# A gated convolution and an MLP on one core: k's first chunk loaded first, kv stored with its time permuted, token transfers merged

## The chip, the core and the metric

The kernel runs on one core of a Trainium2 chip. The metric is the time on the device in microseconds (us). A time in this text is the median of a kernel's executions unless a single one is named. The kernel before ran at 240.22 us (three executions, 240.03 to 240.64) before the change was tried. The state of an execution is "fast" or "slow"; for a kernel that ran once it is unknown. Only fast executions are compared. Where stages are compared, their times come from the profiled execution of each kernel and count from the start of its span.

TensorE does matmuls, VectorE (DVE in the profile), ScalarE (ACT) and GpSimd (POOL) do the elementwise work, and PEld is TensorE's loading of weights. PSUM is the memory that the matmuls of these kernels write to; SBUF holds all their other tiles. The granted clock is the share of TensorE's full clock that the profile shows for a stretch.

## The reference, cut to what matters

All arrays are bf16. x is the input A_q, so its load reads in_A_q_dram in the profile. The sequence has S = 2048 steps and D = 512 channels; the MLP is 1376 wide.

```python
k_shift = sum over t of k_pad[:, t:t+S, :] * shift_k[:, 3-t]     # four taps in time
kv = k_shift * v
y  = irfft(rfft(kv_padded) * rfft(ssm_k_padded))[:, :S]          # long convolution, by channel
y  = y + kv * ssm_D
h  = x + layernorm(x) * y
h2 = h + relu(layernorm(h) @ w1) @ w2
```

## The kernel before

It computes the two Fourier transforms by matmuls in two stages. In order of time it (1) transposes ssm_k and makes tables of sines, (2) makes stage 1 of the transform of ssm_k, in eight blocks, between which TensorE makes the four taps with diagonal weights and VectorE multiplies by v, (3) transposes kv into rows, (4) makes stage 2 for ssm_k ("k spectra"), then stage 1 for kv, (5) multiplies the spectra ("products"), (6) transforms back (psi, then pz, which ScalarE copies to zt), and (7) runs gate, layer norm and MLP over four groups of 512 tokens.

The places that the change touches, with cuts:

```python
def _tokens(src2d, t0, nt):                       # four patterns, 32 rows each
    return [bass.AP(..., offset=... + (16*a + t0)*D, ap=[[64*D, 32], [1, nt*D]]) for a in range(4)]
...
nc.sync.dma_start(out=sk[:], in_=A_ssm_k...)      # first on the queue
... shift_k, ssm_D on ScalarE's queue ...
for c in range(4):                                # then chunks of k and v, transposed
    nc.sync.dma_start_transpose(out=kT[c]..., in_=k_d[...])
    nc.sync.dma_start_transpose(out=vT[:, :, CH*c:CH*c+CH], in_=v_d[...])
...
def to_rows(src, q, fl, eng):                     # 8 transposes: weights with a step of 64 elements
    for i in range(8):
        nc.tensor.transpose(out=pst[:, i, :], in_=src[:, :, :, 8*q + i], identity=ident[:])
...
def taps(u):                                      # u: chunk of 512 steps, group of 128 channels
    ... four matmuls with wdiag into ps ...
    vv = vT[:, rg, CH*c:CH*c+CH]
    nc.vector.tensor_tensor(out=vv, in0=ps[:], in1=vv, op=ALU.mult)        # in place
stage1(kfl, a1k, "ADAADADA", two_taps)            # two units of taps after each block
for q in range(8): to_rows(kvv, q, xfl, ...)      # the kv transposes
for kp in range(16): ... 16 k spectra ...
stage1(xfl, a1x, "ADADADAA")                      # then the transform of kv
...
for a, src in enumerate(_tokens(x_d, 0, NT)):     # four loads of x
    nc.sync.dma_start(out=xh[32*a:32*a+32]..., in_=src)
...
for a, dst in enumerate(_tokens(out_d, t, 1)):    # four stores per 128 tokens
    nc.sync.dma_start(out=dst, in_=o[32*a:32*a+32, :])
```

Of the kernel before, what the change touches and what calls it, by code (L numbers as in the profile page):

```python
# [9 lines left out]
ALU = mybir.AluOpType  # L10
BF16 = mybir.dt.bfloat16
F32 = mybir.dt.float32
F32R = mybir.dt.float32r
I32 = mybir.dt.int32
PSUM = bass.MemoryType.PSUM
P = 128
# [32 lines left out]
def _tokens(src2d, t0, nt):  # L49

    D = src2d.shape[1]
    return [bass.AP(tensor=src2d.tensor, offset=src2d.offset + (16 * a + t0) * D, ap=[[64 * D, 32], [1, nt * D]])
            for a in range(4)]
# [3 lines left out]
def kernel(  # L57
# [37 lines left out]
    nc.sync.dma_start(out=sk[:], in_=A_ssm_k.rearrange("(c p) t -> p c t", p=P))  # L95
    wsh = consts.tile([P, DC, KS], BF16, name="wsh")
    nc.scalar.dma_start(out=wsh[:], in_=A_shift_k.rearrange("(r p) j -> p r j", p=P))
    dtab = consts.tile([P, DC, 64], BF16, name="dtab")
    for dp in range(2):
        src = bass.AP(tensor=A_ssm_D.tensor, offset=A_ssm_D.offset + 64 * dp, ap=[[0, 64], [P, DC], [1, 64]])  # L100
        nc.scalar.dma_start(out=dtab[64 * dp:64 * dp + 64, :, :], in_=src)
# [6 lines left out]
    for c in range(4):  # L108
        if c == 0:
            nc.sync.dma_start_transpose(out=kT[c][:, :, 16:CH + 16], in_=k_d[0:CH, :])  # L110
        else:
            nc.sync.dma_start_transpose(out=kT[c][:], in_=k_d[CH * c - 16:CH * c + CH, :])
        nc.sync.dma_start_transpose(out=vT[:, :, CH * c:CH * c + CH], in_=v_d[CH * c:CH * c + CH, :])
# [21 lines left out]

    n1i = early.tile([P, 1], I32, name="n1i")
# [5 lines left out]
    for s in range(0, P, 64):  # L142
# [5 lines left out]
    ident = consts.tile([P, P], BF16, name="ident")  # L148
    nc.gpsimd.memset(ident[:], 0.0)
    nc.gpsimd.affine_select(out=ident[:], in_=ident[:], compare_op=ALU.not_equal, fill=1.0,  # L150
                            base=0, pattern=[[-1, P]], channel_multiplier=1)

# [9 lines left out]
    _sin(f1f[:, 0:32], t1[:, 0:32], 128)  # L162
    _sin(f1f[:, 32:64], t1[:, 32:64], 128, neg=True)
# [6 lines left out]
    _turns(nc, tsn[:], r2[:], n2c[:], 8192, False)  # L170
# [14 lines left out]
    for rg in range(DC):  # L185
        nc.gpsimd.tensor_tensor(out=wdiag[:, rg, :, :], in0=ident[:].unsqueeze(1).to_broadcast([P, KS, P]),
                                in1=wsh[:, rg, :].unsqueeze(2).to_broadcast([P, KS, P]), op=ALU.mult)
# [5 lines left out]
    def to_rows(src, q, fl, eng):  # L193
        pst = psum.tile([P, 8, P], BF16, tag="ps", name="pst")
        for i in range(8):
            nc.tensor.transpose(out=pst[:, i, :], in_=src[:, :, :, 8 * q + i], identity=ident[:])  # L196
        copy(eng, fl[:, :, :, 8 * q:8 * q + 8], pst[:].rearrange("p i (d g) -> p g d i", d=2))
# [7 lines left out]
    def stage1(fl, a_out, engs, between=None):  # L205
        for gb in range(8):
            pss = [psum.tile([P, 8, 64], F32, tag="ps", name=f"ps1_{r}") for r in range(4)]
            for gi in range(8):
                for f, first in ((f1hi, True), (f1lo, False)):
                    for rg in range(4):  # L210
                        rows = slice(32 * rg, 32 * rg + 32)
                        nc.tensor.matmul(out=pss[rg][:, gi, :],  # L212
                                         lhsT=fl[rows, 8 * gb + gi, :, :].rearrange("p d n -> p (d n)"),
                                         rhs=f[rows, :], start=first, stop=not first, tile_position=(32 * rg, 0))
            for rg in range(4):
                j0 = 64 * rg + 8 * gb
                copy(engs[(4 * gb + rg) % len(engs)], a_out[:, :, j0:j0 + 8], pss[rg][:].rearrange("p g c -> p c g"))
            if between is not None:
                between(gb)

    def stage2(ps, a_in, kp, s):

        for kk in range(2):
            k1 = 2 * kp + kk
            w_re, w_im = ((cc, cs), (cn, cc))[s]
            nc.tensor.matmul(out=ps[:, kk, :], lhsT=w_re[:, k1, :], rhs=a_in[:, k1, :], start=True, stop=False,  # L226
                             skip_group_check=True)
            nc.tensor.matmul(out=ps[:, kk, :], lhsT=w_im[:, k1, :], rhs=a_in[:, 32 + k1, :], start=False, stop=True,  # L228
                             skip_group_check=True)


    kfl = early.tile([P, 64, 2, 64], BF16, name="kfl")
    skv = sk[:].rearrange("p c (a b) -> p c a b", b=64)
    for q in range(8):
        to_rows(skv, q, kfl, "DADADADA"[q])
# [11 lines left out]
    a1k = slotA.tile([P, 64, 256], F32R, tag="A", name="a1k")  # L247


    def taps(u):  # L250
        c, rg = divmod(u, DC)
        ps = psum.tile([P, CH], F32, tag="ps", name="pkv")
        for j in range(KS):
            nc.tensor.matmul(out=ps[:], lhsT=wdiag[:, rg, j, :], rhs=kT[c][:, rg, 16 - j:CH + 16 - j],  # L254
                             start=(j == 0), stop=(j == KS - 1))
        vv = vT[:, rg, CH * c:CH * c + CH]
        nc.vector.tensor_tensor(out=vv, in0=ps[:], in1=vv, op=ALU.mult)

    def two_taps(gb):
        taps(2 * gb)  # L260
        taps(2 * gb + 1)

    stage1(kfl, a1k, "ADAADADA", two_taps)
# [6 lines left out]
    kvv = vT[:].rearrange("p r (a b) -> p r a b", b=64)  # L270
    for q in range(8):
        to_rows(kvv, q, xfl, "ADADADAD"[q])
# [4 lines left out]
    dcol = dtab[:].rearrange("p r g -> p (r g)").unsqueeze(2).to_broadcast([P, 256, 2])  # L277
    for kp in range(16):
        ks = slice(2 * kp, 2 * kp + 2)
        ps = [psum.tile([P, 2, 256], F32, tag="ps", name=f"ps2k{s}") for s in range(2)]  # L280
        for s in range(2):
            stage2(ps[s], a1k, kp, s)
        nc.vector.tensor_tensor(out=kf[:, 0, :, ks], in0=ps[0][:].rearrange("p k j -> p j k"), in1=dcol, op=ALU.add)  # L283
        nc.scalar.copy(out=kf[:, 1, :, ks], in_=ps[1][:].rearrange("p k j -> p j k"))  # L284

    a1x = slotA.tile([P, 64, 256], F32R, tag="A", name="a1x")
    stage1(xfl, a1x, "ADADADAA")
# [15 lines left out]
    def product(kp):  # L303
        ks = slice(2 * kp, 2 * kp + 2)
        kfr = kf[:].bitcast(F32)
        ts = []
        for s in range(2):
            u = psum.tile([P, 2, 256], F32, tag=f"u{s}", name=f"u{s}")
            stage2(u, a1x, kp, s)
            usb = prod.tile([P, 256 - NJ, 2], F32, tag=f"usb{s}", name=f"usb{s}", bufs=2)  # L310
            uj = u[:].rearrange("p k j -> p j k")
            nc.scalar.copy(out=usb[:], in_=uj[:, po, :])  # L312
            t = prod.tile([P, 2, 256, 2], F32R, tag=f"t{s}", name=f"t{s}")
            for eng, in0, j in ((nc.vector, uj[:, dv, :], dv), (nc.gpsimd, usb[:], po)):
                n = j.stop - j.start
                eng.tensor_tensor(out=t[:, :, j, :], in0=in0.unsqueeze(1).to_broadcast([P, 2, n, 2]),  # L316
                                  in1=kfr[:, :, j, ks], op=ALU.mult)
            ts.append(t)
        pending.append((kp, ts))
# [23 lines left out]
    for a, src in enumerate(_tokens(x_d, 0, NT)):  # L343
        nc.sync.dma_start(out=xh[32 * a:32 * a + 32, :, :].rearrange("p t d -> p (t d)"), in_=src)
# [39 lines left out]
    for b in range(32):  # L384
        ps = psum.tile([P, 2, 2 * P], F32, tag="ps", name="psi1")
        for i in range(2):
# [4 lines left out]
        copy("ADAADADA"[b % 8], bp[:, 2 * b:2 * b + 2, :, :, :].rearrange("p g a b c -> p g (a b c)"), ps[:])  # L391
# [9 lines left out]
    pzp = pl.push("psZ", bufs=1, space=PSUM)  # L401
    ptp = pl.push("psT", bufs=1, space=PSUM)
    psum = pl.push("psM", bufs=3, space=PSUM)
# [4 lines left out]
    def inv2(q):  # L408
        pz = pzp.tile([P, 4, 4, P], F32, tag="pz", name="pz")
        for l4 in range(4):  # L410
# [11 lines left out]
    def inv2_copy(q, pz):  # L422
        zts[q] = hp.tile([P, 4, D], BF16, tag="zt", name="zt")
        for l4 in range(4):
# [46 lines left out]
    def chain(q):  # L471
        qln = ln1(q)
# [5 lines left out]
    def mlp1(sc, part=slice(0, 512)):  # L478
# [3 lines left out]
        for fc in range(NFC):  # L482
            fsz = min(P, DFF - fc * P)
# [6 lines left out]
    def mlp2(sc):  # L490
        for i in range(4):
# [8 lines left out]
            for a, dst in enumerate(_tokens(out_d, t, 1)):  # L500
                nc.sync.dma_start(out=dst, in_=o[32 * a:32 * a + 32, :])
# [9 lines left out]
    inv2_copy(0, inv2(0))  # L511
    hln = new_rows(0)
    gate(0, [0, 1], qln, hln, on_act=True)
    gate(0, [2, 3], qln, hln, on_act=True)
    pz = inv2(1)
    transposes(0, hln)
    mlp1(0, slice(0, 2 * P))
    transposes(2, hln)
    inv2_copy(1, pz)
    mlp1(0, slice(2 * P, 4 * P))  # L520
    chain(1)
    inv2_copy(2, inv2(2))
    mlp2(0)
    chain(2)
    mlp1(1)
    inv2_copy(3, inv2(3))
    mlp2(1)
    chain(3)
# [34 lines left out]
```

## Time and profile before

| | before |
|---|---|
| median of the first runs | 240.22 us |
| span of the profiled execution, granted clock | 238.6 us, 0.952 |
| busy: TensorE / VectorE / ScalarE / GpSimd | 86% / 65% / 55% / 26% |
| kv transposes start | 39.71 us |
| first product | 74.73 us |
| first pz (inverse, second half) | 124.99 us |
| first matmul of the MLP | 141.08 us |
| pz of the second group | 154.97 us |
| last add | 234.08 us |

The chain of waits is read as start, length, and what the end of the program was waiting for in that time. In the stretch of the taps, from 21.7 to 36.5 us, it belongs to TensorE alone:

```profile
24.84 1.84 PE pkv L254 x8
26.67 0.61 PE ps L212 x64
27.29 1.84 PE pkv L254 x8
```

Each block costs 1.84 + 0.61 = 2.45 us. VectorE multiplies by v beside it. In the table of groups (line, engine, operation, tiles and shapes, count; busy us, mean ns; idle before it) its sixteen products read:

```profile
L257 DVE TENSOR_TENSOR vT<-pkv,vT 128x512 bf16<-128x512 f32 x16 | 10.7, 689 | 1.2 <-PE pkv L254 1.2
```

### The profile page before, as it was taken

How to read it: one execution, taken by the hardware profiler on the slowest of the kernel's cores; microseconds unless marked ns; L12 is line 12 of the kernel's file. 1: busy time of each engine (PE TensorE's matmuls, PEld its weight loads, DVE VectorE, ACT ScalarE, POOL GpSimd, SP SyncE). 2: the span in 40 equal slices, each digit the busy share in tenths (PEclk: the TensorE clock that was granted, in tenths of full speed). 3: DMA queues.
4: the chain of work that ended last, by engine and by line, in shares of the span. 5: the costliest groups of instructions: out<-in, count | busy, mean ns of one | idle time of the engine just before them, and what ended most of it. 6: DMA issues, size and time to landing. Idle time of an engine off the chain costs nothing.

```text
span 238.6 us, 7218 instructions
## 1 busy us (share of the span) xinstructions
PE 206.1 (86%) x3100; PEld 145.8 (61%) x3100; DVE 154.2 (65%) x299; ACT 130.7 (55%) x241; POOL 62.7 (26%) x88
## 2 busy tenths in 40 slices
PE   0486998999767999998989678899999999979992
PEld 0473555999646999978986546764446444434440
DVE  7886986877655989977995882822577257740031
ACT  3779464666775688897992338912262327105500
POOL 6399700000003999975000001020022002200000
PEclk9999999999955899999999779999999999999998
DMA  6999910000000000009992000023200420042011
GB/s 212 286 206 157 190 34 4 3 1 0 3 5 3 3 1 0 3 1 201 195 368 70 3 3 0 3 46 69 61 8 3 93 71 17 0 91 65 23 44 44
DMA packets 30191, 15.45 MB, mean 65 GB/s; under 512 B 25584, under 2 KB 29008, under 8 KB 30032
## 3 DMA queue, kind: packets, MB, share of 16 engines
q1 hardware_dynamic: 29088, 14.93, 28.3%
q8 instruction: 24, 0.39, 0.7%
q10 hardware_dynamic: 1072, 0.07, 0.4%
q14 instruction: 7, 0.06, 0.1%
HBM read 7.08 MB, written 2.10 MB: 38 GB/s over the span
## 4 chain that ended last, share of the span: by engine, by line
PE 79%; ACT 9%; DMA 5%; DVE 4%; issue 2%; SPq 0%; ACTq 0%
PE ps1m L486 16%; PE ps2m L496 15%; PE pz L417 9%; PE psi L389 6%; PE pst L196 5%; PE psy L326 5%; PE pkv L254 5%; PE u L226 4%; PE u L228 4%; DMA sk<-in_A_ssm_k_dram 4%; PE ps L212 3%; PE ps2k L226 3%; PE ps2k L228 3%; ACT zt L425 2%; ACT c2c L174 2%
## 5 line engine op out<-in xcount | busy, mean ns | idle before, releaser
L488 ACT ACTIVATE h1T<-ps1m 128x512 bf16<-128x512 f32 (+3 forms) x55 | 28.0, 515 | 39.3 <-PE ps1m L486 38.5
L486 PE MATMUL ps1m<-hlnT,w 128*128 128x512 bf16 (+3 forms) x220 | 40.5, 346 | 4.5 <-ACT hlnT L508 2.2
L496 PE MATMUL ps2m<-w,h1T 128*128 128x512 bf16 (+1 forms) x176 | 38.7, 379 | 0.0
L486 PEld LDWEIGHTS <-w 128*128 128x128 bf16 (+1 forms) x220 | 22.6, 103 | 22.1 <-issue 5.3
L499 DVE TENSOR_TENSOR o<-ps2m,xh 128x512 bf16<-128x512 f32 x16 | 11.0, 691 | 38.2 <-PE ps2m L496 38.2
L316 DVE TENSOR_TENSOR t<-u,kf 128x704 fp32r<-128x704 f32 x32 | 27.1, 889 | 4.8 <-ACT usb L312 4.8
L496 PEld LDWEIGHTS <-h1T 128*128 128x128 bf16 (+1 forms) x176 | 17.0, 98 | 21.1 <-issue 0.8
L316 POOL TENSOR_TENSOR t<-usb,kf 128x320 fp32r<-128x320 f32 x32 | 28.7, 924 | 3.4 <-ACT usb L312 2.3
L417 PE MATMUL pz<-bp,ecore 32*32 32x128 f32 x1024 | 22.1, 387 | 4.2 <-ACT zt L425 2.2
L434 POOL TENSOR_SCALAR rstd<-mv 128x4 f32<-128x4 f32 x6 | 1.4, 229 | 88.5 <-DVE mv L441 88.5
L417 PEld LDWEIGHTS pz<-bp,ecore 32*32 32x32 f32 x1024 | 15.8, 108 | 9.8 <-issue 2.9
L439 DVE BATCH_NORM_STATS2 st<-xh 128x6 f32<-128x512 bf16 x32 | 19.8, 680 | 0.0
L328 ACT CAST kf<-psy 128x512 fp32r<-128x512 f32 x32 | 18.4, 645 | 1.6
L389 PE MATMUL psi<-dre,kf 128*128 128x256 f32 x64 | 15.8, 288 | 0.9 <-ACT kf L328 0.9
L425 ACT CAST zt<-pz 128x512 bf16<-128x512 f32 x16 | 8.2, 602 | 13.9 <-PE pz L417 13.9
L326 PE MATMUL psy<-t,ipos 128*128 128x512 f32 x48 | 15.8, 390 | 0.0
L389 PE MATMUL psi<-dim,kf 128*128 128x256 f32 x64 | 15.4, 283 | 0.0
L254 PE MATMUL pkv<-kT,wdiag 128*128 128x512 bf16 x64 | 15.2, 381 | 0.0
L196 PE MATMUL pst<-ident,sk 128*128 128x128 bf16 x64 | 6.7, 299 | 9.2 <-DMA sk<-in_A_ssm_k_dram 9.2
L201 ACT CAST a1k<-ps 128x512 fp32r<-128x512 f32 x20 | 10.4, 593 | 6.7 <-PE ps L212 6.7
L283 DVE TENSOR_TENSOR kf<-ps2k,dtab 128x512 fp32r<-128x512 f32 x16 | 11.0, 694 | 3.5 <-PE ps2k L228 3.4
L284 ACT CAST kf<-ps2k 128x512 fp32r<-128x512 f32 x16 | 10.2, 641 | 5.5 <-PE ps2k L228 5.3
(108 smaller groups left out, 410.0 us busy)
## 6 DMA issues: line engine op xcount, KB each, us to landing
sk<-in_A_ssm_k_dram SPq DMA_DIRECT2D x1, 2048.0 KB, 8.4
xh<-in_A_q_dram SPq DMA_DIRECT2D x4, 512.0 KB, 8.6
out_dram<-o SPq DMA_DIRECT2D x64, 32.0 KB, 1.6
w<-in_B_w_dram SPq DMA_DIRECT2D x1, 1376.0 KB, 15.1
w<-in_B_w_dram SPq DMA_DIRECT2D x1, 1280.0 KB, 18.2
hlnT<-hln SPq DMA_TRANSPOSE x12, 2.5
w<-in_B_w_dram SPq DMA_DIRECT2D x1, 96.0 KB, 17.8
dtab<-in_A_ssm_D_dram ACTq DMA_DIRECT2D x2, 32.0 KB, 8.4
```

The costliest lines, as they stand in the source:

```text
L196: nc.tensor.transpose(out=pst[:, i, :], in_=src[:, :, :, 8 * q + i], identity=ident[:])
L226: nc.tensor.matmul(out=ps[:, kk, :], lhsT=w_re[:, k1, :], rhs=a_in[:, k1, :], start=True, stop=False, skip_group_check=True)
L254: nc.tensor.matmul(out=ps[:], lhsT=wdiag[:, rg, j, :], rhs=kT[c][:, rg, 16 - j:CH + 16 - j], start=(j == 0), stop=(j == KS - 1))
L316: eng.tensor_tensor(out=t[:, :, j, :], in0=in0.unsqueeze(1).to_broadcast([P, 2, n, 2]), in1=kfr[:, :, j, ks], op=ALU.mult)
L326: nc.tensor.matmul(out=psy[:], lhsT=m_[:], rhs=t_.rearrange("p j k -> p (j k)"), start=first, stop=not first)
L328: nc.scalar.copy(out=kf[:, s, :, 2 * kp:2 * kp + 2], in_=psy[:].rearrange("p (j k) -> p j k", k=2))
L389: nc.tensor.matmul(out=ps[:, i, :], lhsT=kf[:, c, 4 * m:4 * m + 4, :].rearrange("p r k -> p (r k)"), rhs=d[:].rearrange("p a b -> p (a b)" ...
L417: nc.tensor.matmul(out=pz[32 * a:32 * a + 32, r4, l4, :], lhsT=ecore[rows, rho, n2, :], rhs=rhs, start=(rho == 0), stop=(rho == 1), tile_p ...
L439: nc.vector.bn_stats(out=st[:, t % 4, :], in_=xh[:, t, :])
L486: nc.tensor.matmul(out=ps1[:fsz, :], lhsT=w1[:, c, fc * P:fc * P + fsz], rhs=hlnTs[sc][:, c, part], start=(c == 0), stop=(c == DC - 1))
L488: nc.scalar.activation(out=h1s[sc][:fsz, fc, part], in_=ps1[:fsz, :], func=ACT.Relu)
L496: nc.tensor.matmul(out=ps2[:], lhsT=h1s[sc][:ksz, fc, i * P:(i + 1) * P], rhs=w2[:ksz, fc, :], start=(fc == 0), stop=(fc == NFC - 1))
```

## The change

The intent: TensorE is idle while ssm_k loads (0 us busy of the first 9.15), so a quarter of the taps is to be done in that time; kv is to be stored so that its transposes load contiguous weights (in the kernel before a load from vT with the step of 64 elements takes 202 ns, one of the contiguous diagonals 98); the diagonals move from GpSimd to VectorE so that they are there early. Beyond that the diff interleaves the transform of kv with the second half of the k spectra (a1 in two halves), gives the inverse transform two half-size buffers, moves layer norms ahead, and merges each group of four token DMAs into one. Its core:

```diff
-    return [bass.AP(..., offset=... + (16 * a + t0) * D, ap=[[64 * D, 32], [1, nt * D]]) for a in range(4)]
+    return bass.AP(..., offset=... + t0 * D, ap=[[16 * D, 4], [64 * D, 32], [1, nt * D]])
...
-    nc.sync.dma_start(out=sk[:], in_=A_ssm_k...)                 # was first
+    nc.sync.dma_start(out=wsh[:], in_=A_shift_k...)              # then k's first chunk, then ssm_k
...
+        nc.vector.tensor_tensor(out=wdiag[:, rg, :, :], in0=ident..., in1=wsh..., op=ALU.mult)   # was gpsimd
...
+    kvx = sk[:]...rearrange("p (b r a) -> p r a b", r=DC, a=32)  # time t = 64*a + b; a innermost
+    kvr = sk[:]...rearrange("p (b x) -> p b x", x=P)             # one transpose: 128 contiguous elements
...
+            nc.vector.tensor_tensor(out=kvx[:, rg, 8 * c:8 * c + 8, :], in0=ps[:].rearrange("p (a b) -> p a b", b=64),
+                                    in1=vv.rearrange("p (a b) -> p a b", b=64), op=ALU.mult)
...
+    first = [taps(u) for u in range(DC)]                         # before the transposes of ssm_k
...
+    for rg in range(DC):
+        nc.gpsimd.tensor_copy(out=kvx[:, rg, 0:8, :], in_=vT[:, rg, 0:CH]...)   # first chunk
...
-        to_rows(kvv, q, xfl, "ADADADAD"[q])
+        to_rows(lambda n2: kvr[:, n2, :], q, xfl, "ADADADAD"[q])
...
+    for gb in range(8):                                          # interleaved
+        stage1(gb, xfl, lambda h, j: a1x[:, h, :, j:j + 8], ...)
+        if gb < 4:
+            spectrum_k(8 + 2 * gb)
+            spectrum_k(9 + 2 * gb)
...
-    for a, src in enumerate(_tokens(x_d, 0, NT)):
-        nc.sync.dma_start(out=xh[32 * a:32 * a + 32, :, :]..., in_=src)
+    nc.sync.dma_start(out=xh[:].rearrange("p t d -> p (t d)"), in_=_tokens(x_d, 0, NT))
...
+    pzp = pl.push("psZ0", bufs=2, space=PSUM)                    # inverse in half-size steps
...
+            nc.sync.dma_start(out=_tokens(out_d, t, 1), in_=o[:])  # one store, was four
```

The time of the permuted store is split as t = 64a + b, with a from 0 to 31. An element of kv lies at position 128b + 32r + a, where r is the group of channels. A product of one chunk covers eight values of a and all 64 of b, and runs through b first. So its neighbouring results lie 128 elements, which is 256 bytes, apart.

## The prediction

> **What bounds the kernel now.** I read the clock and busy slices first, then the chain that ended last in order of time, then single tiles and the timelines of VectorE and ScalarE around each gap of that chain. TensorE is 79% of the chain and 86% busy, so the question at each stage is where it waits. The chain of waits in order of time (start us, length us, what):
>
> ```profile
> 0.72 8.38 DMA sk<-in_A_ssm_k_dram
> 9.15 6.76 PE pst L196 x64
> ...
> 16.95 3.98 ACT c2c L174 x2
> ...
> 39.71 6.00 PE pst L196 x64
> ...
> 72.15 2.54 ACT a1x L201 x5
> ...
> 131.31 2.06 ACT zt L425 x4
> ...
> 149.01 1.96 ACT zt L425 x4
> ...
> 212.29 2.45 DMA hlnT<-hln
> ...
> 234.08 0.69 DVE o L499
> ```
>
> Every line that is not PE is time in which TensorE waits: 9.15 us for ssm_k; 4 us for ScalarE's second sine table; 2.5 us (and, before it, the copies of the x transform from 61.1 to 72.1) for the evacuation of a1x; twice 2 us for zt; 2.45 us for the last transposed hlnT; and the stores after the last sum at 234.8, with the span ending at 238.6. In windows of the stretch around the x transform (window, length; PE, PEld, DVE, ACT, POOL busy with counts; granted clock; DMA share, GB/s):
>
> ```profile
> 62.00:64.00 2.00, 1.34 (x88) 0.85 (x71) 1.77 (x3) 2.00 (x5) 0.00 (x0) 1.00 0.03 8
> 66.00:68.00 2.00, 0.77 (x30) 0.48 (x29) 0.96 (x2) 1.58 (x4) 0.00 (x0) 0.50 0.00 0
> 120.00:122.00 2.00, 2.00 (x19) 2.00 (x18) 1.97 (x6) 1.78 (x4) 0.00 (x0) 1.00 1.04 394
> ```
>
> TensorE is under half busy at 66 us and its clock has been halved. The third line is for a transfer rate that I need below. Weights that load from vT with a step of 64 elements against contiguous diagonals, from the views of the two tiles (ns min/median/max):
>
> ```profile
> L196 PEld LDWEIGHTS <-vT x64: 172/202/221, 39.7 to 45.4; 128*128 128x128 bf16 x64
> ```
>
> ```profile
> L254 PEld LDWEIGHTS <-wdiag x64: 95/98/99, 17.6 to 38.3; 128*128 128x128 bf16 x64
> ```
>
> [...] 0.50 from about 66 to 79 us, and the first 24 products' matmuls come every 0.21 us where later ones take 0.12. [...] The new pattern has 4 as its slowest DRAM dimension against 128 partitions[...]. Nothing in the trace of before shows such a DMA; this is my largest doubt.
>
> **The change part by part.** The diff holds much more than its title.
>
> (a) Front. shift_k and k's first chunk go ahead of ssm_k on the one queue. ssm_k now takes 8.4 us from 0.72; a k chunk (0.5 MB) landed about 2.5 us after it. So I put ssm_k at 12.3 and k's first chunk near 6, and v's first chunk, behind both in either order, stays near 14.8. The sixteen first taps (4 x 0.92 = 3.7 us of TensorE, from the pitch of 1.84 us per two units) fit between 7 and 12, when it was idle. Against that, VectorE now makes the diagonals (4 x about 0.5, by the 0.42 us of a plain 128x512 bf16 product), so the first table's turns end near 10 instead of 7.1, and ScalarE's table (4.2) ends near 14.3. The eight sk transposes run 12.3 to 20.2, held up by four banks that the first taps keep until v's first chunk lands and VectorE multiplies (4 x 0.65, to 18.7); the last kfl copy ends near 21.5, where it was 16.9. ScalarE's second table then runs 20.4 to 24.5, the same stall as before but later, and TensorE restarts at about 25.4. Twelve units and six blocks are left: 1.84 + 5 x 2.45 + 0.61 = 14.7, so the last block ends at 40.2 and the kv transposes start at 40.4, 0.7 later than now. They are contiguous: 64 at some 57 ns (eight pt transposes take 0.62 us with their drain) is 3.7 us for 6.0. The k spectrum starts at 44.1 instead of 45.7: **-1.6**. GpSimd copies the first chunk by about 30, long before it is needed.
>
> (b) Spectra and the x transform interleaved. Now: 16 x 0.96 = 15.4 of spectrum, bound by TensorE, then 11.0 of x transform bound by copies, then 2.5 of tail, in all 29 us to 74.7. After: 8 spectra 7.7; four blocks of one transform step and two spectra, each 2 x 0.65 + 2 x 0.67 = 2.65 on VectorE (TensorE 0.61 + 1.93 = 2.54), 10.7; the last four steps with 10 copies on ScalarE at 0.505, 5.2; tail 0.5. That is 24.1: **-4.9**. The layout of a1 in halves is what allows it; no wait is added, as each half is free by then.
>
> (c) Clock. The thin stretch shrinks from 11 to some 5.5 us, which may or may not trip the halving. It cost 24 x 0.09 = 2.2 us, but GpSimd (0.92 x 32 = 29.6 busy of 33.3) then sets the pace. I count **-0.5**.
>
> (d) Front of the inverse. With two buffers of four banks and halves, zt, gate and transforms overlap. From the first pz at 0: halves end at 3.1, 6.2, 9.3, 12.3; gate of tokens 0,1 runs 4.2 to 7.2; zt of 2,3 waits in ScalarE's order for that gate's root (7.5 to 8.6); second gate to 11.6; zt of the second group 11.9 to 14.0; the new small pools overlie those banks, so the pt transposes start at 13.0 and the first MLP at 15.1, against 16.1 now. Then its two halves run without the 1.5 + 2.3 us of waits between them: 6.4 + 0.6 + 5.1 ends at 27.2 against 30.0: **-2.8**.
>
> (e) The last chain. Its first layer norm (2.46 + 0.36 + 1.5 + 1.38 us) moves ahead of the adds of the second MLP, so hlnT is there by 209 where it now holds TensorE from 213.5 to 214.9: **-1.4**.
>
> (f) Stores. The last four issues of 0.42 become one: **-1.0** at the tail.
>
> The sum is -12.2: 228.0 us.
>
> (g) The token DMAs on fewer engines. In the view of the tile, the old load reads so:
>
> ```profile
> L344 SPq DMA_DIRECT2D xh<-in_A_q_dram x4: 354/416/421, 107.2 to 108.6; - x4
> ...
> DMA to landing us min/median/max: 5.5/8.6/11.5
> ```
>
> All four land by about 120, 4 us before VectorE first reads xh at 124.2. On 4 engines: 394 GB/s over 16 is 24.6 each in the weights' window, so 2.1 MB takes 21 us plus 1.5. Issued at about 100.3 (seven earlier) it lands at 123, and VectorE wants it at 117.2; the whole chain of (d) moves by some 5. The last store would take 1.3 us longer at 32 KB an engine and eat (f). That is +5.9: 234 us. [...] I give it 45%[...], because a kernel that is already tuned is unlikely to keep a load that makes its next stage wait.
>
> **The rivals.** First, (g): a transfer that was hidden becomes the wait. For: [...]the shrinking slack. Against: 4 us of slack today, and four DMAs into 32 partitions each reached only some 230 GB/s, which one of 128 partitions on all engines could better. It makes 234. Second, VectorE and ScalarE become the bound of the front: the table is later by 3 us, [...]and the kfl copies alternate behind both. For: ScalarE's 4 us is on the chain already and everything queues in order. Against: TensorE gets 3.7 us of taps done early and has 14.7 us of its own left. If ssm_k lands at 13.5 or the order bites harder, the front loses 2 instead of gaining 1.6: 231 to 232 without (g), 237 with it. Third, TensorE is already so busy that gaps only move: in the product stage GpSimd and TensorE are both nearly full, so a better clock is worth nothing, and the first MLP starts cold again; that takes some 2 off (c) and (d): 230.
>
> **How range and chances follow.** Without (g) I hold 228 with a spread of about 2.5, with it 234 with about 3. Weighted this is 230.7, and I round up to 231. The tenth lowest and highest of that mixture lie near 226 and 237. Faster by 2% means under 235.4: nearly certain without (g), some two thirds with it, hence 0.86. Slower needs several stalls at once.
>
> **What would show it.** (a) kfl's last copy near 21.5, kv transposes starting near 40.4 with weight loads near 100 ns and lasting under 4.5 us. (b) the first product near 68 with VectorE nearly full from 52 to 62. (c) the clock's halved slices gone or fewer. (d) no zt line of 2 us in the chain in front of the first MLP; (e) no hlnT DMA in it. (f) one store at the end. (g) xh landing over 18 us after its issue and a wait of VectorE's statistics for it. The prediction is wrong if the kv transposes start after 43, if xh is late by more than 8 us, or if the interleaved blocks take over 3.2 us each because PSUM banks run out.

## The result and the profile after

The kernel after takes 276.94 us (four executions, 275.99 to 277.24); the kernel before in the same rounds takes 240.22 (three executions, 240.03 to 240.64). A fourth of it, 243.92, is over 1.5% above the fastest, so it counts as slow and is left out; with it the median is 240.43. The ratio is 1.152, with a 95% interval of 1.148 to 1.156: it is slower by 15%. Ratios here are the mean time of one kernel's fast runs over that of the other's of the same rounds, so they are not quite the ratio of the medians quoted. The profiled execution has a span of 274.8 us at a mean clock of 0.888.

The stages show where the time came from (us from the start of the span):

| start of | before | after | added in this stage |
|---|---|---|---|
| kv transposes | 39.71 | 58.85 | +19.1 |
| first product | 74.73 | 90.49 | −3.4 |
| first pz | 124.99 | 140.22 | −0.5 |
| first matmul of the MLP | 141.08 | 179.09 | +22.8 |
| last add | 234.08 | 269.40 | −2.7 |
| end of span | 238.6 | 274.8 | +0.9 |

Two stages lost 42 us, the others together gained 5.7. The chain of waits of the kernel after has pieces of another kind than before:

```profile
3.41 10.09 DMA sk<-in_A_ssm_k_dram
...
27.05 4.76 DVE sk L252 x2
31.82 0.52 DVE a L205
...
38.06 4.62 DVE sk L252 x2
...
58.85 5.76 PE pst L198 x64
...
122.48 40.51 DMA xh<-in_A_q_dram
163.01 2.47 DVE st L469 x4
...
174.94 1.94 ACT zt L455 x4
...
269.40 0.69 DVE o L530
```

Between 27 and 58 us the chain now runs through VectorE: two products that hold it for 4.6 to 4.8 us, then a copy, then the next products. Later a single DMA of 40.5 us stands in it. The groups say the same of the product, and that the transposes' weights did become cheaper (L198 mixes the 64 loads for ssm_k, still with a step, and the 64 for kv; its shortest load takes 97 ns, where the shortest with the step took 168 in the kernel before):

```profile
L252 DVE TENSOR_TENSOR sk<-pkv,vT 128x512 bf16<-128x512 f32 x12 | 28.3, 2545 | 1.1 <-PE pkv L242 1.1
...
L198 PEld LDWEIGHTS <-sk 128*128 128x128 bf16 x128 | 11.5, 166 | 5.1 <-issue 4.1 <-DMA sk<-in_A_ssm_k_dram 1.0
```

The product takes 2545 ns on the same shapes that took 689, and VectorE waited only 1.1 us before the twelve of them, so it sets the pace. The table of waits (who waited for whom: us in total, times, longest) has the other loss:

```profile
DVE st L469 <- DMA xh<-in_A_q_dram: 23.5, 1, 23.5
PE pz L445 <- ACT zt L455: 22.8, 2, 20.8
```

VectorE's first statistics stand 23.5 us for the load of x, and TensorE stands 20.8 us in one piece behind it, because the gate, and then ScalarE's zt, come in that order. In windows (start and end, length; busy us and count of PE, PEld, DVE, ACT, POOL; granted clock; DMA share; GB/s) of both stretches:

```profile
24.00:26.00 2.00, 0.62 (x2) 0.29 (x3) 1.99 (x4) 1.77 (x5) 2.00 (x2) 0.50 1.15 144
150.00:154.00 4.00, 0.00 (x0) 0.00 (x0) 0.00 (x0) 0.00 (x0) 0.00 (x0) 0.50 0.25 66
```

In the second every engine is idle, the DMA share is 0.25, and 66 GB/s move. In the first TensorE is short of work (0.62 us busy of 2.00) and its clock is at 0.50. That the 40.5 us are one transfer is seen in the view of the tile:

```profile
L372 SPq DMA_DIRECT2D xh<-in_A_q_dram x1: 732/732/732, 122.5 to 122.5; - x1
```

### The profile page after: what moved, and what is told of

The parts are those of the page before. It is cut to its first block, busy times and chain, and to the rows that moved or that the text cites. A ratio compares the mean times of both kernels' runs of the same rounds, so it can differ in the third digit from the quotient of the medians.

```text
span 274.8 us, 7155 instructions
## 1 busy us (share of the span) xinstructions
PE 210.0 (76%) x3087; PEld 146.7 (53%) x3100; DVE 176.0 (64%) x307; ACT 129.7 (47%) x239; POOL 67.3 (24%) x88
## 4 chain that ended last, share of the span: by engine, by line
PE 55%; DMA 18%; DVE 18%; ACT 3%; issue 3%; SPq 1%; POOLq 0%; DVEq 0%; ACTq 0%
DMA xh<-in_A_q_dram 15%; PE ps1m L517 14%; PE ps2m L527 14%; DVE sk L252 9%; PE psy L355 5%; PE pz L445 4%; DMA sk<-in_A_ssm_k_dram 4%; PE u L229 3%; PE ps2k L229 3%; PE u L231 3%; PE pst L198 3%; PE ps2k L231 3%; DVE a L205 2%; DVE st L469 2%; PE ps L214 2%
## 5 line engine op out<-in xcount | busy, mean ns | idle before, releaser
L445 PE MATMUL pz<-bp,ecore 32*32 32x128 f32 x1024 | 21.8, 389 | 25.2 <-ACT zt L455 22.8
L469 DVE BATCH_NORM_STATS2 st<-xh 128x6 f32<-128x512 bf16 x32 | 19.8, 680 | 23.5 <-DMA xh<-in_A_q_dram 23.5
L203 ACT CAST a<-ps 128x512 fp32r<-128x512 f32 x38 | 19.8, 596 | 22.6 <-PE ps L214 22.5
L252 DVE TENSOR_TENSOR sk<-pkv,vT 128x512 bf16<-128x512 f32 x12 | 28.3, 2545 | 1.1 <-PE pkv L242 1.1
L242 PE MATMUL pkv<-kT,wdiag 128*128 128x512 bf16 x58 | 19.3, 473 | 9.1 <-DVE wdiag L173 7.1
L205 DVE CAST a<-ps 128x512 fp32r<-128x512 f32 x26 | 17.9, 732 | 3.5 <-PE ps L214 3.5
L214 PE MATMUL ps<-f_hi,kfl 32*128 32x64 bf16 x256 | 8.0, 207 | 12.3 <-DVE sk L252 8.3
L242 PEld LDWEIGHTS <-wdiag 128*128 128x128 bf16 x64 | 6.8, 115 | 18.2 <-DVE wdiag L173 7.4
```

Source lines behind the costliest of these rows:

```text
L203: nc.scalar.copy(out=o, in_=i)
L205: nc.vector.tensor_copy(out=o, in_=i)
L242: nc.tensor.matmul(out=ps[:], lhsT=wdiag[:, rg, j, :], rhs=kT[c][:, rg, 16 - j:CH + 16 - j], start=(j == 0), stop=(j == KS - 1))
L252: nc.vector.tensor_tensor(out=kvx[:, rg, 8 * c:8 * c + 8, :], in0=ps[:].rearrange("p (a b) -> p a b", b=64), in1=vv.rearrange("p (a b) -> ...
L445: nc.tensor.matmul(out=pz[32 * a:32 * a + 32, r4, l4, :], lhsT=ecore[rows, rho, n2, :], rhs=rhs, start=(rho == 0), stop=(rho == 1), tile_p ...
L469: nc.vector.bn_stats(out=st[:, t % 4, :], in_=xh[:, t, :])
```

## The experiments

My theory had two causes that add up: the merged load of x runs on 4 of the 16 DMA engines (the share of 0.25 above; that its slowest dimension of 4 makes it so was an estimate until run 2), and the permuted store makes VectorE the bound of the taps' stretch (2545 ns for a product). The rivals were that the load is slow for another reason than its outer dimension, that the taps' stretch is late because of the new order of the front (ssm_k later, first taps holding PSUM, diagonals on VectorE), and that the product is slow because of how it reads, or by the number of runs it writes, rather than for writing single bf16. Thirteen kernels ran: four on one chip, eight on a second, and the last on a third. The fast executions of the kernel before have a median of 241.26 beside runs 1 to 4, of 239.63 and 239.95 beside the others, and of 240.22 beside the kernel after, so a difference between sessions is good to about 1 us.

**1. The load of x in four again.** This is the kernel after with one edit:

```diff
-    nc.sync.dma_start(out=xh[:].rearrange("p t d -> p (t d)"), in_=_tokens(x_d, 0, NT))
+    for a in range(4):
+        nc.sync.dma_start(out=xh[32 * a:32 * a + 32, :, :].rearrange("p t d -> p (t d)"),
+                          in_=bass.AP(tensor=x_d.tensor, offset=x_d.offset + 16 * a * D, ap=[[64 * D, 32], [1, NT * D]]))
```

> The changed kernel with only xh's load put back to four DMAs of 32 rows. Theory 'four engines': the load is slow because its slowest DRAM dimension is 4, so it runs on 4 of 16 engines. Then xh lands about 9 to 12 us after its issue at 122.5 instead of 40.5, the DMA share after 146 us is near zero, VectorE's statistics no longer wait, the first MLP starts some 15 us after the first pz (140.2) instead of 39, and the time falls by 22 to 24 us to 253 to 255. Rival 'contention': xh is slow because w1 and w2 are loaded beside it; then it lands as late as before and the time stays near 277.

Measured: 252.83 us (ratio 1.049, 1.043 to 1.055). The wait for x is gone: the statistics start at 139.2, before the first pz at 140.0. The edit is worth 276.94 − 252.83 = 24.1 us, about the 23.5 us that VectorE had waited (by the two ratios, each to its own kernel before, it is 24.7).

**2. One load, its DRAM dimensions exchanged.** Same bytes, same single DMA, but 32 as the slowest dimension in place of 4. Rows land in the wrong partitions, so the result is wrong.

```diff
+    nc.sync.dma_start(out=xh[:].rearrange("p t d -> p (t d)"),
+                      in_=bass.AP(tensor=x_d.tensor, offset=x_d.offset, ap=[[64 * D, 32], [16 * D, 4], [1, NT * D]]))
```

> Wrong result on purpose: the same single DMA of the same 128 rows of 16 KB into the same 128 partitions, but with the DRAM dimensions of 4 and 32 exchanged, so 32 is the slowest. Theory 'four engines': 16 engines, DMA share near 1 while it runs, xh lands within 8 to 12 us of its issue, time 251 to 255. Rival 'one DMA of long rows': a single DMA over 128 partitions with 16 KB rows is slow whatever the order; then it lands after some 40 us and the time stays near 277.

Measured: 253.58 us in one run, of unknown state, and no wait for x. The window while x loads:

```profile
124.00:126.00 2.00, 2.00 (x19) 2.00 (x19) 1.97 (x5) 1.92 (x4) 0.66 (x1) 1.00 0.99 426
```

The share is 0.99 where it was 0.25. In the packet records of the kernel after, from 150 to 154 us, there are four packets in flight at 97% of the moments and five at the rest, never fewer; in the kernel before, from 110 to 112, with four loads and a share of 1.06, sixteen to eighteen. One packet counted as one engine, as in the share, that is four of the 16 at work at a time; which four, the records do not say. Merging four loads into one was not the fault; the slowest dimension of 4 was (276.94 us with 4, 253.58 with 32). This one load even moved 426 GB/s where the four of the kernel before moved 213 (110 to 112 us). Why isn't shown, and no run loads the right rows this way.

**3. The permuted store in runs of eight.** The kernel after, with the loops of the product exchanged: a now runs first, so it writes eight neighbours before it steps by 256 bytes. It reads both inputs with a step of 64 elements instead.

```diff
-            nc.vector.tensor_tensor(out=kvx[:, rg, 8 * c:8 * c + 8, :], in0=ps[:].rearrange("p (a b) -> p a b", b=64),
-                                    in1=vv.rearrange("p (a b) -> p a b", b=64), op=ALU.mult)
+            nc.vector.tensor_tensor(out=kvx[:, rg, 8 * c:8 * c + 8, :].rearrange("p a b -> p b a"),
+                                    in0=ps[:].rearrange("p (a b) -> p b a", b=64),
+                                    in1=vv.rearrange("p (a b) -> p b a", b=64), op=ALU.mult)
```

> The changed kernel with the loops of the kv product exchanged: each of the 64 columns is written as a run of 8 adjacent bf16, and both inputs are now read with steps of 64 elements. Same bytes, same instructions. Theory 'scattered writes': each 2-byte write into another 256-byte row costs about 4.7 ns, so with runs of 8 the product falls from 2.55 to 0.7 us, the kv transposes start near 41 instead of 58.9 and the time falls by 15 to 18 us to 259 to 262. Rival 'three-dimensional patterns or reads': the product stays at 2.5 us or more since its reads are now the scattered ones; time 277 or more. Second rival 'GpSimd contention': no change either.

```profile
L252 DVE TENSOR_TENSOR sk<-pkv,vT 128x512 bf16<-128x512 f32 x12 | 12.0, 1036 | 2.9 <-PE pkv L242 2.9
```

Measured: 259.23 us (ratio 1.075), 17.7 less than the kernel after, with the load of x left slow. The kv transposes start at 43.22 and take 3.73 us. So the order of the front is not what made them start at 58.85.

**4. kv in place, as before.** The kernel after without the permuted store: products in place in vT, transposes with the step of 64.

```diff
-    for rg in range(DC):
-        nc.gpsimd.tensor_copy(out=kvx[:, rg, 0:8, :], in_=vT[:, rg, 0:CH].rearrange("p (a b) -> p a b", b=64))
...
-                times_v(u, taps(u))
+                times_v(u, taps(u), place=True)
...
-        to_rows(lambda n2: kvr[:, n2, :], q, xfl, "ADADADAD"[q])
+        to_rows(lambda n2: kvv[:, :, :, n2], q, xfl, "ADADADAD"[q])
```

> The changed kernel with the time-permuted store undone: every kv product goes in place into vT, GpSimd's four copies go, and the transposes read vT with a step of 64 elements as in the kernel before. Theory: all of the front's loss is the store, so the products take 0.69 us, the kv transposes start near 40.5, their 64 take 6.0 us against 5.8, and the time is 259 to 262. If the early taps, the later ssm_k or VectorE's diagonals cost something of their own, the transposes start later than 43 and the time is over 263.

Measured: 259.52 us (ratio 1.080). The product is back to 688 ns, the kv transposes start at 41.86 and take 5.94 us with weight loads of 202 ns. The permuted store as written is worth 276.94 − 259.52 = 17.4 us of loss. What the new order of the front alone does is now visible too: 41.86, against 39.71 to 41.22 in three traces with the old order (the kernel before and runs 8 and 12), so it gains nothing here.

**5. The permuted store in pairs.** With the load of x in four (as in 1), and pairs of neighbours in a written together. An aligned pair of bf16 fills a word of 4 bytes; a product still writes 256 separate runs.

```diff
+            nc.vector.tensor_tensor(out=kvx[:, rg, 8 * c:8 * c + 8, :].rearrange("p (a l) b -> p a b l", l=2),
+                                    in0=ps[:].rearrange("p (a l b) -> p a b l", l=2, b=64),
+                                    in1=vv.rearrange("p (a l b) -> p a b l", l=2, b=64), op=ALU.mult)
```

> On top of the four loads of xh, the kv product writes its columns as 256 runs of 2 adjacent bf16 (one aligned 4-byte word each) per 512 elements; the shipped loop writes 512 runs of one element (2.55 us), the earlier experiment 64 runs of eight (1.04 us). Theory 'every run costs': the extra over 0.69 us goes with the number of runs, about 3.6 ns each, so 0.69 + 256 x 3.6 ns = 1.6 us. Rival 'half-word writes': only writes of less than a 4-byte word are slow, so pairs take 0.7 to 1.0 us. Time between 238 and 246.

```profile
L252 DVE TENSOR_TENSOR sk<-pkv,vT 128x512 bf16<-128x512 f32 x12 | 8.2, 690 | 3.5 <-PE pkv L242 3.5
```

Measured: 236.06 us in one run, of unknown state. The product costs 690 ns, as if it were contiguous, though it still jumps 256 bytes after each pair. The theory that every run costs has fallen: halving the number of runs did not halve the excess, it removed all of it. TensorE is back at its pace in the chain of this kernel:

```profile
36.77 0.61 PE ps L214 x64
...
39.22 0.61 PE ps L214 x64
```

39.22 − 36.77 = 2.45 us per block, as before.

**6. Both mended, first form.** Load in four as in 1, runs of eight as in 3.

```diff
+    for a in range(4):                                           # as in 1
+        nc.sync.dma_start(out=xh[32 * a:32 * a + 32, :, :]..., in_=...)
...
+            nc.vector.tensor_tensor(out=kvx[:, rg, 8 * c:8 * c + 8, :].rearrange("p a b -> p b a"), ...)   # as in 3
```

> The changed kernel with both faults mended: xh in four loads and kv written in runs of 8. If the two losses found so far are separate and are all of it, the time is the changed kernel's 277 less 24 and less 17.7, 235 us. If they overlap (the late xh hides part of the front's loss), it is above 240.

Measured: 238.18 us, the kernel before 239.63 (ratio 0.992, 0.987 to 0.996). The two losses add nearly: by simple sum 276.94 − 24.1 − 17.7 = 235.1 was due; this kernel is 3 above it and run 5, at 236.06, 1 above, of which the change of chip may be 1. With both mended the change is at or under the time of the kernel before, so there is no third loss of size.

**7. The stores in four as well.** The kernel of 6 with the four old stores:

```diff
-            nc.sync.dma_start(out=_tokens(out_d, t, 1), in_=o[:])
+            for a in range(4):
+                nc.sync.dma_start(out=bass.AP(tensor=out_d.tensor, offset=out_d.offset + (16 * a + t) * D,
+                                              ap=[[64 * D, 32], [1, D]]), in_=o[32 * a:32 * a + 32, :])
```

> As the mended kernel, and the output stores too put back to four of 32 rows. Theory 'four engines' holds for stores as well: with 16 engines the last store lands about 1 us sooner after its issue, but four issues of 0.42 cost 1.3 more, so the tail from the last add to the end goes from 4.7 to about 4 and the time falls by 0.3 to 1. Rival: one issue is always better, so the time rises by about 1.

Measured: 237.43 us (ratio 0.988, 0.983 to 0.993). From the start of the last add to the end of the span it takes 4.5 us, where the single store of 6 takes 4.97. The medians differ by 0.75 us, the intervals overlap; the end of the span is the surer sign.

**8. The title undone.** Kernel 7 with ssm_k first, no leading taps, kv in place and diagonals on GpSimd, so that what is left of the change is the interleaving, the halves of the inverse and the moved layer norms.

```diff
+    nc.sync.dma_start(out=sk[:], in_=A_ssm_k...)                 # first again
-    first = [taps(u) for u in range(DC)]
-        if 0 < gb < 7:
-            for u in (2 * gb + 2, 2 * gb + 3):
-                times_v(u, taps(u))
+            for u in (2 * gb, 2 * gb + 1):
+                times_v(u, taps(u), place=True)
```

> The changed kernel with everything of its title undone (ssm_k first, taps of the first chunk in their old place, kv in place in vT with strided transposes, diagonals on GpSimd) and with loads and stores in fours, so that only the interleaved spectra, the halves of the inverse and the earlier layer norms stay. The plain-store run had its kv transposes start at 41.9 where the kernel before has 39.7, so the theory that the new front order itself costs 2 us gives a start at 39.7 and the first product at 70.5 to 71, and a time of 234 to 236. If the new front order is neutral, the time equals the mended kernel with four stores within 1 us.

Measured: 236.21 us (ratio 0.984, 0.980 to 0.989). This is no worse than kernel 7, which has the whole title with the runs of eight (the intervals overlap). The kv transposes of its profiled execution start at 41.22 rather than the 39.71 of the kernel before; its clock was at 0.56 to 0.59 from 22 to 26 us, where the kernel before has 1.00. Run 12, with the same front but for the store and the transposes of kv, has 1.00 as well. What decides whether the dip comes is not shown.

**9. Four forms of the write, side by side.** One kernel with the load in four, in which each group of channels writes its products in another form. The data of kv is wrong. The comparison with the reference passed all the same, I take it because the convolution's part of the output is small beside x; only the lengths of the products are used.

```diff
+            if rg == 0:    # single bf16 every 4 bytes
+                o = skf[:, 0:1024].rearrange("p (a b x) -> p a b x", a=8, x=2)[:, :, :, 0]
+            elif rg == 1:  # single bf16 every 64 bytes
+                o = skf[:, 0:2048].rearrange("p (b a) -> p a b", a=32)[:, 0:8, :]
+            elif rg == 2:  # contiguous write, both inputs read with a step of 64 elements
+                o = skf[:, 0:512].rearrange("p (b a) -> p b a", a=8)
+            else:          # runs of four every 256 bytes
+                o = kvx[:, rg, 8 * c:8 * c + 8, :].rearrange("p (a l) b -> p a b l", l=4)
```

> Wrong result on purpose: the twelve later kv products write in four forms, one for each group of channels, from its own source line: (0) single bf16 every 4 bytes; (1) single bf16 every 64 bytes; (2) adjacent bf16 in order, but both inputs read with a step of 64 elements; (3) runs of four adjacent bf16 every 256 bytes. Theory 'half-word writes': a bf16 written alone in its 4-byte word is slow whatever the step, so forms 0 and 1 take about 2.5 us, form 3 about 0.7, and form 2 about 1.0, which would be the part that the runs of eight paid for their reads. Rival 'wide step': the 256-byte step is the cost, so form 0 takes 0.7 and form 1 between 0.7 and 2.5. Rival for the runs of eight, 'long runs cost': form 2 takes 0.7.

```profile
L259 DVE TENSOR_TENSOR sk<-pkv,vT 128x512 bf16<-128x512 f32 x3 | 7.2, 2402 | 0.9 <-PE pkv L242 0.7
L266 DVE TENSOR_TENSOR sk<-pkv,vT 128x512 bf16<-128x512 f32 x3 | 3.1, 1030 | 0.3
L262 DVE TENSOR_TENSOR sk<-pkv,vT 128x512 bf16<-128x512 f32 x3 | 3.0, 1007 | 0.0
...
L256 DVE TENSOR_TENSOR sk<-pkv,vT 128x512 bf16<-128x512 f32 x3 | 2.2, 725 | 9.2 <-POOL sk L279 9.2
```

The lines are, in order, every 64 bytes, runs of four, strided reads, every 4 bytes. A single every 4 bytes costs next to nothing (725 ns for 689), one every 64 bytes nearly as much as one every 256 (2402 for 2545). Reading both inputs with the step costs 1007 by itself, so the 1036 of runs of eight is a cost of reading, not of writing, and so is the 1030 of runs of four. The pairs of run 5 read with the same step, two elements at a time, and pay nothing (690); why is not shown. (One run, 248.44 us.)

**10. The slow load put into the kernel before.** The kernel before with only the load of x merged, with 4 as slowest dimension.

```diff
-    for a, src in enumerate(_tokens(x_d, 0, NT)):
-        nc.sync.dma_start(out=xh[32 * a:32 * a + 32, :, :].rearrange("p t d -> p (t d)"), in_=src)
+    nc.sync.dma_start(out=xh[:].rearrange("p t d -> p (t d)"),
+                      in_=bass.AP(tensor=x_d.tensor, offset=x_d.offset, ap=[[16 * D, 4], [64 * D, 32], [1, NT * D]]))
```

> The kernel before with one part of the change alone: xh loaded by one DMA with 4 as its slowest DRAM dimension. Theory 'four engines': it lands some 40.5 us after its issue near 107.3, so at about 148, 23.6 us after VectorE wants it (124.2); the pz of the first group and the second cannot hide that, so the time is 240 + 20 to 24, 260 to 264. Rival 'the old order hides it': under 250.

```profile
DVE st L439 <- DMA xh<-in_A_q_dram: 23.5, 1, 23.5
```

Measured: 262.36 us in one run (state unknown), against 239.95: that part alone costs some 22 us. It was issued at 109.3, where the old loads of x started at 107.2, and the first statistics that need it start at 149.8. The same wait of 23.5 us arises in a kernel with nothing else changed.

**11. The whole change, mended.** Kernel 5 with the stores in four: the title stays, with pairs in place of singles.

```diff
+        nc.sync.dma_start(out=xh[32 * a:32 * a + 32, :, :]..., in_=...)                        # as in 1
+            nc.vector.tensor_tensor(out=kvx[...].rearrange("p (a l) b -> p a b l", l=2), ...)   # as in 5
+                nc.sync.dma_start(out=..., in_=o[32 * a:32 * a + 32, :])                       # as in 7
```

> The changed kernel with its title's parts kept and three things mended: xh in four loads, kv written in pairs, stores in fours. From the single look at pairs (236.1, one store) and the 0.75 us that four stores gave the runs-of-eight kernel: 235 to 236, faster than before by about 2%. If four stores do not help, 236.

Measured: 234.89 us (six executions, 234.0 to 235.83; ratio 0.979, 0.975 to 0.982).

**12. The old front with the permuted store in pairs.** Kernel 8 with the permuted store in pairs and contiguous transposes:

```diff
-                times_v(u, taps(u), place=True)
+                times_v(u, taps(u))                              # pairs, into kvx
...
-        to_rows(lambda n2: kvv[:, :, :, n2], q, xfl, "ADADADAD"[q])
+        to_rows(lambda n2: kvr[:, n2, :], q, xfl, "ADADADAD"[q])
```

> As the last, but with ssm_k first, no leading taps and diagonals on GpSimd as in the kernel before: only the time-permuted store (in pairs) is left of the title. If contiguous transposes are worth the 2.2 us that 64 of them save (5.97 to 3.73) on top of the old front's 236.2, the time is 234. If the new front's early taps are worth something once the store is cheap, this one is slower than the last.

Measured: 234.65 us (six executions, 234.19 to 235.33; ratio 0.978, 0.974 to 0.982). It is the fastest of all, beats both kernels, and is as fast as kernel 11 within the spread. So the early chunk of k, the leading taps and the diagonals on VectorE bring nothing that shows, and the permuted store in pairs brings 236.21 − 234.65 = 1.6 us (the executions of the two kernels do not overlap, the intervals of their ratios just do, and they ran in different rounds). Runs 6, 7, 8, 11 and 12 are all faster than the kernel before, their intervals lying under 1; by 2%, none of them is beyond doubt. A part of why the early taps bring nothing shows in the same window of kernel 11 and then of kernel 12:

```profile
24.00:26.00 2.00, 0.95 (x2) 0.41 (x3) 1.67 (x3) 2.00 (x5) 2.00 (x2) 0.50 0.73 145
```

```profile
24.00:26.00 2.00, 1.95 (x71) 1.09 (x71) 1.77 (x4) 0.98 (x3) 2.00 (x3) 1.00 1.34 241
```

With the early taps ScalarE's second table comes later (it starts at 19.67 in kernel 11, at 16.97 in kernel 12), TensorE is idle from 19.4 to 21.9 us in kernel 11, and its clock is at 0.50 when the blocks start. The kernel after and runs 4, 5 and 6, also with the new front, have 0.50 in this window too. In the old order TensorE is at work with a clock of 1.00 by then in the kernel before and in kernel 12, but not in run 8 (0.56), so the clock is no full answer.

**13. More steps, and pairs across words.** As 9, with other forms; again only the lengths count.

```diff
+            if rg == 0:    # single every 8 bytes
+                o = skf[:, 0:2048].rearrange("p (a b x) -> p a b x", a=8, x=4)[:, :, :, 0]
+            elif rg == 1:  # single every 16 bytes
+                o = skf[:, 0:4096].rearrange("p (a b x) -> p a b x", a=8, x=8)[:, :, :, 0]
+            elif rg == 2:  # single every 32 bytes
+                o = skf[:, 0:8192].rearrange("p (a b x) -> p a b x", a=8, x=16)[:, :, :, 0]
+            else:          # pairs as in 5, shifted by one element: each lies across two words
+                o = skf.rearrange("p (b r a) -> p r a b", r=DC, a=32)[:, rg, 8 * c - 1:8 * c + 7, :]
```

> Wrong data on purpose, as in the forms run (there the comparison with the reference still passed). Single bf16 written every 8 bytes, every 16 and every 32, and pairs of adjacent bf16 at an odd element, so that each pair lies across two 4-byte words. Known so far: single every 4 bytes 0.73 us, every 64 bytes 2.40, every 256 bytes 2.55, aligned pairs every 256 bytes 0.69. Theory 'partial word, each in a line of its own': a half-filled word is cheap while its neighbours in the same 32 or 64 bytes follow, and dear when each write is in a new one; then 8 bytes takes under 1.2 us, 16 in between or low, 32 about 1.5 to 2.4, and the odd pairs, two half-filled words each, about 2.4 or more. Rival 'number of runs or step alone': the odd pairs take 0.7 as the aligned ones do.

```profile
L259 DVE TENSOR_TENSOR sk<-pkv,vT 128x512 bf16<-128x512 f32 x3 | 7.3, 2429 | 0.3
L262 DVE TENSOR_TENSOR sk<-pkv,vT 128x512 bf16<-128x512 f32 x3 | 6.9, 2316 | 0.0
L265 DVE TENSOR_TENSOR sk<-pkv,vT 128x512 bf16<-128x512 f32 x3 | 5.2, 1717 | 0.1
...
L256 DVE TENSOR_TENSOR sk<-pkv,vT 128x512 bf16<-128x512 f32 x3 | 3.9, 1297 | 8.8 <-POOL sk L279 8.8
```

In order: every 16 bytes, every 32, shifted pairs, every 8. The excess over 690 ns is 0.6 us at 8 bytes and 1.6 to 1.9 from 16 bytes on, where the lengths are nearly level: 2429, 2316, 2402 and 2545 ns at 16, 32, 64 and 256 bytes (this run, run 9 and the kernel after). Spread over the 512 singles of a product, an estimate, these are 4.5 to 5.0 ns each; at 8 bytes it is 2.5 (1297 / 512), at 4 bytes 1.4 (725 / 512), and in order 1.3 (689 / 512). The 4.7 ns expected for run 3 is the shortest such product of the kernel after, 2404 / 512. Aligned pairs, which fill whole words, cost nothing here (690 ns every 256 bytes). The shifted pair shows that the place in the words counts, and neither runs nor reads: the same pairs, read alike and written one element off, cost 1717 instead of 690. Why a half-filled word costs more, and more as the step grows to 16 bytes, no trace shows. (One run, 255.74 us.)

## Why the prediction was wrong, and where it was right

It predicted 231.0 (226 to 237) and faster; the kernel is slower, at 276.94. Two of the three marks that it named for its own failure came true: the kv transposes start after 43 (at 58.85), and x is late by more than 8 us (by 23.5). The third, interleaved blocks of over 3.2 us, did not (2.72).

**(a), the front: wrong, by the cost of the product.** The step that failed is "Twelve units and six blocks are left: 1.84 + 5 x 2.45 + 0.61 = 14.7". Up to it the working held: ssm_k was due at 12.3 and landed at 13.5, but the last kfl copy was due near 21.5 and ended at 21.85, and TensorE restarted at 25.15 for 25.4. The 2.45 is the pitch of the kernel before and holds only while VectorE keeps up with products of 0.69 us. The working kept it for the twelve later products although their output pattern had changed to single bf16 every 256 bytes. They measured 2.55. A block then costs two products and the copies of stage 1 on VectorE: 38.06 to 48.96 in the chain is two blocks, 5.45 us each. The blocks took from 25.15 to 58.72, which is 33.6 us, for 14.7. The prediction had itself set 202 ns against 98 for the weights that load with a step and without, but gave the product that now wrote with one no cost. The store moved the stepping walk from TensorE's loads to VectorE's writes (2545 ns for 689). The contiguous transposes did come out as said: 3.73 us for 3.7 in run 3. In the kernel after itself they took 5.76, with the clock at 0.50 for most of it (from 58 to 62 us; 0.71 from 62 to 64).

Even with the product mended, (a) is not there. In run 5 the six blocks run from 25.18 to 41.68, 16.5 us for 14.7; they begin at half clock (0.50 from 24 to 26 us) and come down to a pitch of 2.45 us, and in run 11 the kv transposes start at 41.56 for 40.4. Run 12, with the old order, has them at 40.55. The second rival, "VectorE and ScalarE become the bound of the front", had the right place, for a reason it did not give.

**(g), the load of x: the right cause, its size and its chance wrong.** That the load would run on four engines was an estimate, for which the trace of before showed nothing. The share of 0.25 and the four packets in flight bear it out, and run 2 shows that the dimension decides it (share 0.99 with 32). The mis-sized term is "24.6 each": it came from a window in which sixteen engines were busy at 394 GB/s (share 1.04). Four engines alone moved 66 (share 0.25), which is 16.5 each. The transfer took 40.5 us where the term gave 22.5 (21 plus 1.5, an estimate; the 32 KB stores of the kernel before take 1.6 us from issue to landing). Over its whole length the mean is 2,097,152 bytes / 40.51 us = 51.8 GB/s, less than the 66 of the late window. It was slower beside the weights, queued behind it: the trace's 16 KB packets, the length of x's rows, landed at 47 GB/s from 126 to 140 us, while the weights moved too (share 0.98 to 1.14), and at 65.5 from 142 to 158, when they were through (share 0.26). At 66 GB/s throughout the 2,097,152 bytes would have taken 31.8 us; from the first packet's start to the last landing it was 38.4, so the slower stretch cost some 6.6 by this estimate. Why four engines moved 16.5 each where sixteen moved 26.6 each (run 2) is not shown. The step of judgement that failed is that "a kernel that is already tuned is unlikely to keep a load that makes its next stage wait": it gave 45% to an estimate that runs 1, 2 and 10 bore out in kind. In the kernel after, where (a)'s loss moved the start of the load from the 100.3 foreseen to 122.5 but moved its consumer as well, it cost 24.1 us (run 1); alone in the kernel before, 22 (run 10).

**(b), the interleaved spectra: right in kind, its tail mis-sized.** From the end of the kv transposes to the first product it took 29.0 us before, 25.9 after (64.6 to 90.5) and 25.3 in run 12 (44.30 to 69.58), for the 24.1 predicted: a gain of 3.1 to 3.7 for 4.9. The four interleaved blocks take 2.72 us each for 2.65. What failed is "tail 0.5": ScalarE's last five copies stand in front of the first product as they did before (2.54 us there), in the kernel after and, by its chain, in run 12:

```profile
87.91 2.54 ACT a L203 x5
```

**(c), the clock: nil.** The halved stretch shrank (from 65.6 to 79.3 us before, from 87.0 to 93.9 after), but the clock is still at 0.50 when the products start, and the first products' matmuls are 0.21 us apart as before, for a gain of 0.5.

**(d), the front of the inverse: nil for −2.8.** From the first pz to the pz of the second group it takes 30.0 us before (124.99 to 154.97) and 30.1 in run 12 (120.10 to 150.21), where nothing waits for x. The failed step is "the new small pools overlie those banks, so the pt transposes start at 13.0 and the first MLP at 15.1". In the chain of run 12:

```profile
120.10 4.43 PE pz L441 x190
...
133.90 1.08 ACT zt L451 x2
...
135.02 1.03 PE pt L535 x8
...
137.19 4.43 PE ps1m L513 x20
```

The transposes start 14.9 after the first pz, directly behind ScalarE's last two copies of zt, and the MLP at 17.1, where it was 16.1 before. Its first 20 matmuls take 4.43 us, 0.22 each, twice the 0.11 of the same matmuls in the kernel before at full clock (32 in 3.65 us): the third rival, that "the first MLP starts cold again", is what happened, if cold means the halved clock. The kernel before has 0.50 there as well (142 to 144 us), but in run 12 the clock stays at 0.50 from about 133.5 to 143. The waits between the halves of the MLP did go, and it takes 13.0 us for 13.9, which just pays for the later start.

**(e), the last chain: right.** From the pz of the second group to the last add it takes 79.1 us before (154.97 to 234.08) and 77.4 in run 12 (150.21 to 227.57): −1.75 for −1.4.

**(f), the stores: wrong sign.** From the last add to the end it takes 4.5 us before and in run 7 with four stores, and 4.97 (run 6) to 5.4 (after) with one. (g) had foreseen it in a sentence, "The last store would take 1.3 us longer", an estimate from 24.6 GB/s for an engine; with the issues that it saves, the one store came out 0.5 to 0.9 us longer.

The sum, by runs: the load of x +24.1, the permuted store +17.4 to +17.7, and the rest −5.1 (kernel 11, whose edits mend the two and undo the merged stores, is at 234.89, against 239.95 of the kernel before). 24.1 + 17.5 − 5.1 = 36.5, and 276.94 − 240.22 = 36.7; with sessions that differ by 1 us, this is as near as it can be. The gain of about 5 that the change holds, mainly (b) and (e), was there all along, under two losses.

What stays open: why reading both inputs with a step of 64 elements adds 0.3 us, and not when it is done in pairs; why half-filled words cost more (2429 ns every 16 bytes for 690 in aligned pairs); what decides whether the clock dips at 22 to 26 us in the old front (0.56 to 0.59 in run 8, 1.00 in run 12); and why a DMA engine moved less when four worked than when sixteen did (16.5 GB/s for 26.6).

## What to carry to other kernels

A layout that makes one engine's reads contiguous may have scattered another engine's writes: give that write its own duration, and if it is bf16, order its loops so that it fills whole 4-byte words (here 690 ns in aligned pairs, 2545 in singles). When DMAs are merged, look at the slowest dimension of the new DRAM pattern before you count the issues saved (here a share of 0.25 with 4, 0.99 with 32). Where an estimate says that a part will be bad, weigh it by the slack that the trace shows (here 4 us, and the wait was 23.5). That the kernel looks tuned is no evidence against it.
